# Local and pooled attention with a mixture layer on one core: eight output steps in whole float32, weight casts on another engine, and a planner with new rules

## The chip, the cores and the metric

The kernel runs on one core of one Trainium2 chip. Its engines work in parallel, each through its own queue in order: TensorE (PE, matmuls; PEld is its weight load), VectorE (DVE), ScalarE (ACT), GpSimd (POOL, which also issues the adding DMAs) and SyncE (SP, which issues the other DMAs). The metric is the device time of one execution in microseconds, as the median of several runs. Lower is better.

## The reference: what is computed

```python
# q, k, v: 8 batches, 8 heads, 576 tokens, 64 values
q_d, k_d, v_d = means over groups of 4 tokens                     # 144 pooled tokens
out_up = repeat(softmax(q_d k_d^T / 8) v_d, 4)                    # pooled attention
out_local = softmax(q k^T / 8 where |i - j| < 4) v                # local attention
x = (out_up + out_local), heads side by side                      # 4608 x 512
h = x @ w_in                                                      # 512 x 2048
P = a0 + a1 h + a2 h^2 + a3 h^3
Q = 1 + |b0| |h| + |b1| h^2
out = (P / (Q + 1e-6)) @ w_out                                    # 2048 x 512
```

Everything is float32.

## The kernel before, in words

**Attention.** A pair is two heads of a batch, so a batch is four pairs. For each pair the kernel multiplies q and k in ten windows of 58 tokens (L409) and for the pooled tokens (L426), takes exponentials on ScalarE (L456, L482), normalizes, turns the weights (L530, L537), multiplies them with v (L579, L568) and adds the two results into x, stored transposed (L611).

**The layer.** Tokens are taken in ten blocks: eight of 512 tokens, one batch each, and two that gather the last 64 tokens of four batches. The first block has 16 steps. A step takes 128 of the 2048 columns: it multiplies x with a chunk of w_in into a PSUM bank (`h_part`), ScalarE and VectorE form the rational function g = P / Q (`middle`), and two steps later g is multiplied with a chunk of w_out, into four banks that collect over the steps (`o_part`). A float32 value is split into a high part of reduced precision and a rest, and a product is three matmuls: high x high, rest x high, high x rest. Only the first block's product with w_in, L680, is done in whole float32, since the splits aren't ready there. `middle` forms 1/Q as exp(-ln Q), multiplies (L729) and then finds the rest of g in three further operations (L732, L737, L738).

**The weights.** Both matrices come as 32 chunks of 512 KB. Each is loaded into a buffer (a "spot"), scaled on ScalarE (L320), put together from two words on VectorE (L323, L326), and then split by `parts`: GpSimd rounds it to the high part (L340), VectorE subtracts to get the rest (L343). For w_out this happens directly after the decoding. The spots lie over memory whose owner isn't in use yet; there are five for the first chunks, four that rotate, and two more.

**What sets the order.** A planner: every piece of work is a task with an engine, a cost, what it reads and writes, and sometimes a due time. The planner works out for each task how late it may start, and then runs the engines in time. On each engine it takes, of the tasks whose inputs are there, the one that may start latest the soonest. The order that results is each engine's program. So constants such as `H0`, `H_FIRST` and `SPLIT_EARLY` are wishes that set the order; they are no waits. Before the first product, TensorE is given matmuls without use (L889) where the plan has it idle.

In the first block everything meets: batch 0's attention, the loading and splitting of both matrices, the 16 steps, and batch 1's attention, whose x the second block needs. From the second block on, a step is 24 matmuls on TensorE, and the attention of a later batch is woven in.

Of the kernel before, what the change touches and what calls it, by code (L numbers as in the profile page):

```python
# [72 lines left out]
class Task:  # L73
    __slots__ = ("engine", "dur", "fn", "due", "preds", "succs", "late", "start", "end", "n", "lag")


class Plan:

    LAG = {"PE": 0.25, "DVE": 0.14, "ACT": 0.18, "POOL": 0.2, "SP": 2.0}
    OWN = {"PE": 0.0, "DVE": 0.08, "ACT": 0.1, "POOL": 0.1, "SP": 2.0}
# [6 lines left out]
    def add(self, engine, dur, fn, reads=(), writes=(), due=None, lag=None):  # L89
        t = Task()  # L90
        t.engine, t.dur, t.fn, t.due, t.n = engine, dur, fn, due, len(self.tasks)
        t.lag, t.preds, t.succs, t.late, t.start = lag, {}, [], 1e9, None
# [11 lines left out]
        for k in rk - wk:  # L104
            self.readers[k].append(t) if k in self.readers else self.readers.__setitem__(k, [t])
# [62 lines left out]
def attention_moe(  # L168
# [95 lines left out]
    slots += [Slot(2 + i, high[i][half].at) for i in range(2)]  # L264
    vf = put("vf", [KC, NPAIR, 2, 2, D], F32, low[0][half].at)
# [3 lines left out]
    spots += [put(f"sl{i}", [P, 2 * DM], I32, a[w][NFC - 2].at) for i, (a, w) in enumerate(((high, 0), (low, 0), (high, 1), (low, 1)))]  # L269
    spots += [put(f"sx{i}", [P, 2 * DM], I32, xs[1][0].at + i * 4096) for i in range(2)]  # L270
# [34 lines left out]
    def weights(w, f, spot, due=None):  # L305
# [25 lines left out]
        add("SP", 1.4, load, (), (spot,), due=due)  # L331
# [3 lines left out]
        if w:  # L335
            parts(w, f)

    def parts(w, f, due=None):
        hi, lo, word = high[w][f], low[w][f], bits[w][f]
        add("POOL", 1.0, lambda: nc.gpsimd.tensor_copy(out=hi.ap, in_=word.ap.bitcast(F32)), (lo,), (hi,), due=due)  # L340
# [19 lines left out]
    def load_qk(c, due=None):  # L360
        s, b, i = c.slot, c.b, c.i
        add("SP", 1.6, lambda: nc.sync.dma_start(out=s.qk.ap, in_=qk[b, i]), (), (s.qk,), due=due)

# [4 lines left out]
    def load_pooled(c):

        s, b, i = c.slot, c.b, c.i  # L370
        for dst, src, cost in ((s.pq, qkp, 0.5), (c.vp, vp, 0.4)):
            add("SP", cost, lambda d=dst, x=src: nc.sync.dma_start(out=d.ap, in_=x[b, 0, :, i]), (), (dst,))
            for r in range(1, POOL):
                add(
                    "POOL", 1.0,
# [15 lines left out]
    def scores(c, bk):  # L391
# [24 lines left out]
        add("PE", 1.0, issue, (s.qk, identb, maskb), bk)  # L416

    def scores_pooled(cs, bk):
# [14 lines left out]
        add("PE", 0.9, issue, [c.slot.pq for c in cs], bk)  # L433
# [548 lines left out]
```

## Time and profile before

| what | value |
|---|---|
| median of 3 runs | 995.44 us (995.34 to 995.81) |
| span of the profiled execution | 992.7 us (its first to its last instruction; the timed runs' median is 2.7 us above it) |
| TensorE busy | 961.0 us, 97% |
| VectorE busy | 849.1 us, 86% |
| ScalarE busy | 796.6 us, 80% |
| GpSimd busy | 180.4 us, 18% |
| TensorE busy in 0 to 50, 50 to 100, 200 to 250 us | 35.0, 44.2, 50.0 us |
| VectorE busy in the same stretches | 35.4, 47.6, 44.8 us |
| mean granted TensorE clock | 0.995 |

The page gives the profiled execution by its span; what lies around the span is read as the difference to the median. A matmul on float32 operands appears as two records, so the 64 matmuls of L680 are 128 records. The ends of matmuls are modelled, and a matmul that waits in the array counts as busy; the cost of one is read from the distance between starts.

### The profile page before, as it was taken

To read this page: it belongs to the slowest core of one execution; us is meant where nothing else is said; L and a number is where in the kernel's file an instruction comes from. 1 tells how busy PE (TensorE), PEld (TensorE's weight loads), DVE (VectorE), ACT (ScalarE), POOL (GpSimd) and SP (SyncE) were. 2 spreads that over 40 slices of the span, in tenths; PEclk is the share of its full clock that TensorE was granted. 3 is DMA by queue.
4 is the path that set the end of the run, shared out by engine and by line. 5 is a ranking of instruction groups with operands and counts; after the bars stand their busy time and mean duration, and the time that the engine had idled before them with its cause. 6 is when DMAs were issued, how large, how long until landed. Compare 5 with 4: busy or idle time off the path is not lost.

```text
span 992.7 us, 19799 instructions
## 1 busy us (share of the span) xinstructions
PE 961.0 (97%) x7365; PEld 758.1 (76%) x7365; DVE 849.1 (86%) x1472; ACT 796.6 (80%) x2046; POOL 180.4 (18%) x209
## 2 busy tenths in 40 slices
PE   6689998999999999999999999999999999999997
PEld 5545665788888878987878887887878888898886
DVE  6799999989778988887887898888888898888886
ACT  6578768797979798779787988798797979767675
POOL 1523543222221213001303030302122220000000
PEclk9999999999999999999999999999999999999999
DMA  9963553433342324002424242533334320100001
GB/s 322 281 210 120 118 158 70 117 68 74 74 125 51 74 74 84 34 22 74 75 72 96 85 80 59 95 96 56 92 57 112 74 52 1 44 1 22 1 1 42
DMA packets 46371, 83.43 MB, mean 84 GB/s; under 512 B 6564, under 2 KB 29092, under 8 KB 46276
## 3 DMA queue, kind: packets, MB, share of 16 engines
q1 hardware_dynamic: 25828, 62.70, 19.1%
q0 software_dynamic: 20448, 19.48, 14.1%
q8 instruction: 58, 0.95, 0.4%
q14 instruction: 37, 0.30, 0.1%
HBM read 72.72 MB, written 9.44 MB: 83 GB/s over the span
## 4 chain that ended last, share of the span: by engine, by line
PE 82%; DVE 10%; DMA 4%; issue 2%; POOL 1%; SPq 1%; ACT 1%; ACTq 0%; DVEq 0%; POOLq 0%
PE psum L757 36%; PE psum L692 36%; PE psum L568 2%; DMA pq<-in_qkp_dram 2%; PE psum L579 1%; PE psum L530 1%; PE psum L537 1%; PE psum L409 1%; PE psum L426 1%; DMA qk<-in_qk_dram 1%; DVE m L720 1%; DMA sx<-in_w_out_dram 1%; DVE m L726 1%; POOL wh L340 1%; DVE g L729 1%
## 5 line engine op out<-in xcount | busy, mean ns | idle before, releaser
L757 PE MATMUL psum<-wh,g 128*128 128x512 f32 x1152 | 371.7, 403 | 4.7 <-DVE g L738 2.7
L692 PE MATMUL psum<-xs,wh 128*128 128x512 f32 (+1 forms) x1152 | 265.2, 370 | 0.0
L705 ACT ACTIVATE m<-psum,cf 128x512 f32<-128x512 f32 x288 | 217.5, 759 | 51.9 <-PE psum L692 41.9
L757 PEld LDWEIGHTS psum<-wh,g 128*128 128x128 f32 x1152 | 209.3, 188 | 55.5 <-issue 7.7
L692 PEld LDWEIGHTS psum<-xs,wh 128*128 128x128 f32 x1152 | 199.3, 188 | 35.9
L757 PE MATMUL psum<-wl,g 128*128 128x512 f32 x576 | 225.0, 392 | 0.0
L705 ACT ACTIVATE gb<-psum,cf 128x512 f32<-128x512 f32 x144 | 115.7, 803 | 53.9 <-PE psum L757 53.7
L376 POOL DMA_DIRECT2D pq<-in_qkp_dram x84 | 73.9, 913 | 398.3 <-DMA pq<-in_qkp_dram 312.5
L692 PE MATMUL psum<-xs,wl 128*128 128x512 f32 (+1 forms) x576 | 141.5, 367 | 0.0
L729 DVE TENSOR_TENSOR g<-m,m 128x512 fp32r<-128x512 f32 x144 | 100.6, 699 | 43.2 <-ACT m L705 41.3
L720 DVE SCALAR_TENSOR_TENSOR m<-m,cf,m 128x512 f32<-128x512 f32 x144 | 108.9, 756 | 31.2 <-ACT m L705 31.1
L757 PEld LDWEIGHTS psum<-wl,g 128*128 128x128 f32 x576 | 108.4, 188 | 23.4
L456 ACT ACTIVATE el<-psum,nm 128x64 f32<-128x64 f32 x320 | 97.0, 345 | 30.4 <-DVE nm L448 30.1
L726 DVE TENSOR_TENSOR m<-m,gb 128x512 f32<-128x512 f32 x144 | 101.7, 706 | 20.3 <-ACT gb L705 16.3
L692 PEld LDWEIGHTS psum<-xs,wl 128*128 128x128 f32 x576 | 101.3, 189 | 18.9 <-issue 1.2
L705 ACT ACTIVATE gb<-m,cf 128x512 f32<-128x512 f32 x144 | 107.0, 743 | 6.3 <-DVE m L720 6.3
L732 DVE SCALAR_TENSOR_TENSOR m<-m,g 128x512 f32<-128x512 f32 x144 | 100.0, 695 | 2.9
L737 DVE TENSOR_TENSOR m<-m,m 128x512 f32<-128x512 f32 x144 | 99.2, 689 | 2.8
L376 POOL DMA_DIRECT2D vp<-in_vp_dram x84 | 72.7, 925 | 154.5 <-DMA vp<-in_vp_dram 136.8
L725 DVE TENSOR_TENSOR m<-m,m 128x512 f32<-128x512 f32 x144 | 98.5, 684 | 0.5 <-ACT m L705 0.5
L738 DVE TENSOR_TENSOR g<-m,m 128x512 fp32r<-128x512 f32 x144 | 97.9, 680 | 0.8
L705 ACT ACTIVATE m<-gb 128x512 f32<-128x512 f32 x144 | 93.6, 650 | 3.5 <-DVE m L725 0.9
(66 smaller groups left out, 999.0 us busy)
## 6 DMA issues: line engine op xcount, KB each, us to landing
qk<-in_qk_dram SPq DMA_DIRECT2D x32, 590.0 KB, 8.0
pq<-in_qkp_dram POOLq DMA_DIRECT2D x84, 144.0 KB, 3.3
vw<-in_vw_dram SPq DMA_DIRECT2D x32, 320.0 KB, 4.0
out_dram<-xf SPq DMA_DIRECT2D x32, 256.0 KB, 2.4
vp<-in_vp_dram POOLq DMA_DIRECT2D x84, 72.0 KB, 3.0
sl<-in_w_in_dram SPq DMA_DIRECT2D x10, 512.0 KB, 4.7
sl<-in_w_out_dram SPq DMA_DIRECT2D x10, 512.0 KB, 6.3
pq<-in_qkp_dram SPq DMA_DIRECT2D x28, 144.0 KB, 2.2
```

The costliest lines, as they stand in the source:

```text
L376: lambda d=dst, x=src, r=r: nc.gpsimd.dma_start(out=d.ap, in_=x[b, r, :, i], accum_op=ALU.add),
L456: nc.scalar.activation(out=s.el.ap[:, k, c.pos(j), :], in_=view[:, j, k, :], func=AF.Exp, bias=nm[:, 5 * j + k : 5 * j + k + 1], scale=sca ...
L692: nc.tensor.matmul(ph.ap[:, f * t : (f + 1) * t], lhsT=(high, low)[j][0][fc].ap[:, c, :], rhs=blk.x[i].ap[:, c, :], start=(part_ == 0 and ...
L705: add("ACT", cost, lambda: nc.scalar.activation(out=out_.ap, in_=in_, func=func, **kw), (room_in, cf, *more), (out_,))
L720: lambda: v.scalar_tensor_tensor(out=tb.ap, in0=tq.ap, scalar=b1, in1=tb.ap, op0=ALU.mult, op1=ALU.add),
L725: add("DVE", 0.61, lambda: v.tensor_tensor(out=ta.ap, in0=ta.ap, in1=tq.ap, op=ALU.mult), (ta, tq), (ta,))
L726: add("DVE", 0.61, lambda: v.tensor_tensor(out=ta.ap, in0=ta.ap, in1=u.ap, op=ALU.add), (ta, u), (ta,))
L729: add("DVE", 0.61, lambda: v.tensor_tensor(out=gh.ap, in0=ta.ap, in1=tq.ap, op=ALU.mult), (ta, tq), (gh,))
L732: lambda: v.scalar_tensor_tensor(out=tb.ap, in0=tb.ap, scalar=CONE, in1=gh.ap.bitcast(F32), op0=ALU.add, op1=ALU.mult),
L737: add("DVE", 0.61, lambda: v.tensor_tensor(out=tb.ap, in0=ta.ap, in1=tb.ap, op=ALU.subtract), (ta, tb), (tb,))
L738: add("DVE", 0.61, lambda: v.tensor_tensor(out=gl.ap, in0=tb.ap, in1=tq.ap, op=ALU.mult), (tb, tq), (gl,))
L757: nc.tensor.matmul(ob[sub].ap, lhsT=g[i].ap[:, f0 : f0 + P], rhs=flat((high, low)[j][1][fc].ap), start=(fc == 0 and m == 0), stop=(fc == N ...
```

## The change

1. **Eight output steps in whole float32** (`WHOLE = 8`). In the first eight steps of the first block `middle` takes exp(-ln Q) as a first value of the reciprocal, refines it by one Newton step (two operations), and multiplies P with it: three operations after the reciprocal in place of four, with one float32 result in `u`. `o_part` multiplies it with the unsplit chunk of w_out, one float32 matmul for each of the four groups of 128 tokens in place of three. The first eight chunks of w_out are split after that, for the second block.
2. **The rounding of weights** moves from GpSimd (L340) to ScalarE.
3. **The planner** has a new rule: before it starts a task, it looks for a more urgent one that becomes ready while that task would run, and then holds the engine free or runs only what fits (`HOLD`, until `HOLD_UNTIL`). Loads have a landing time by their size. Many constants change.
4. **Batch 0** goes pair by pair through its attention, in place of two pairs at a time, with banks from a table (`FIRST`). Its pooled values of v are loaded into two buffers of two parts each, in place of one with four additions in a row, so L579's product has four terms in place of two there. Loads have no due times: all of batch 0 first, then the weights. Batch 1's loads are held back in the plan (`HOLD_LOADS`).
5. **Spots.** The two additional ones are gone, and the four rotating ones lie elsewhere.

```diff
     def parts(w, f, due=None):
-        add("POOL", 1.0, lambda: nc.gpsimd.tensor_copy(out=hi.ap, in_=word.ap.bitcast(F32)), (lo,), (hi,), due=due)
+        add("ACT", 0.5, lambda: nc.scalar.copy(out=hi.ap, in_=word.ap.bitcast(F32)), (lo,), (hi,), due=due)
...
-        if w:
+        if w and f >= WHOLE:
             parts(w, f)
...
         act(0.54, tq, log, log.ap, AF.Exp, scale=-1.0)
+        if n < WHOLE:
+            add("DVE", 0.61, lambda: v.scalar_tensor_tensor(
+                    out=tb.ap, in0=tb.ap, scalar=CONE, in1=tq.ap, op0=ALU.add, op1=ALU.mult), (tb, tq), (tb,))
+            add("DVE", 0.61, lambda: v.scalar_tensor_tensor(
+                    out=tq.ap, in0=tb.ap, scalar=2.0, in1=tq.ap, op0=ALU.subtract, op1=ALU.mult, reverse0=True
+                ), (tb, tq), (tq,))
+            add("DVE", 0.61, lambda: v.tensor_tensor(out=u.ap, in0=ta.ap, in1=tq.ap, op=ALU.mult), (ta, tq), (u,))
+            return
...
     def o_part(n, f):
+        if n < WHOLE:
+            x = gb[n % 2]
+            for sub in range(blk.nsub):
+                def issue(sub=sub):
+                    nc.tensor.matmul(
+                        ob[sub].ap, lhsT=x.ap[:, sub * P : (sub + 1) * P], rhs=flat(bits[1][fc].ap).bitcast(F32),
+                        start=(fc == 0), stop=False,
+                    )
+                add("PE", 0.858, issue, (x, low[1][fc]), (ob[sub],), due=due + 0.02 * sub)
+            return
...
-            t = heapq.heappop(open_[e])[2]
+            t = ready[e][0][2]
+            urgent = None
+            for r, _, w in waiting[e]:
+                if r < at + t.dur * HOLD and w.late < t.late - HOLD_MARGIN and (urgent is None or w.late < urgent[0]):
+                    urgent = w.late, r
+            if urgent is not None and at < HOLD_UNTIL:
+                fits = [x for x in ready[e] if at + x[2].dur <= urgent[1] + 0.05]
+                if not fits:
+                    free[e] = urgent[1]
+                    continue
...
-H0 = 40.0
-H_FIRST = 8.0
+H0 = 36.0
+H_FIRST = 6.73
...
-SPLIT_EARLY = 6.0
+SPLIT_EARLY = 9.51
+PARTS_EARLY = 14.42
+PAIR_GAP = 3.53
+HOLD = 0.7
+HOLD_MARGIN = 2.06
+HOLD_UNTIL = 54.4
+WHOLE = 8
+HOLD_LOADS = (45.0, 75.0)
```

How this moves instructions shows best at the end of batch 0's attention. First ScalarE's queue, ahead of step 0 of the first block (L705 before, L720 now, whose first row reads the bank with h). `sl` and `sx` rows are scalings of loaded weights, `up` the pooled result of a pair, `ept` and `et` its turned weights. Before:

```order
L320 ACTIVATE sx0_233<-sx0_233 128x512
L543 COPY ept3_221<-psum 72x288 x2
L553 COPY et3_220<-psum 128x512
L554 COPY et3_220<-psum 128x128
L625 ACTIVATE up0_191<-psum 128x144
L625 ACTIVATE up1_192<-psum 128x144
L320 ACTIVATE sl1_230<-sl1_230 128x512
L320 ACTIVATE sl3_232<-sl3_232 128x512
L320 ACTIVATE sl2_231<-sl2_231 128x512
L320 ACTIVATE sl0_229<-sl0_229 128x512
L320 ACTIVATE sx1_234<-sx1_234 128x512
L705 ACTIVATE m2_166<-psum,cf_181 128x512
```

Now:

```order
L557 COPY ept3_221<-psum 72x288 x2
L567 COPY et3_220<-psum 128x512
L568 COPY et3_220<-psum 128x128
L334 ACTIVATE sl3_233<-sl3_233 128x512
L354 CAST wh1_2_74<-wb1_2_125 128x512
L354 CAST wh1_3_75<-wb1_3_127 128x512
L640 ACTIVATE up1_192<-psum 128x144
L334 ACTIVATE sl2_232<-sl2_232 128x512
L354 CAST wh1_4_76<-wb1_4_129 128x512
L334 ACTIVATE sl1_231<-sl1_231 128x512
L720 ACTIVATE m2_166<-psum,cf_181 128x512
```

Of the five scalings that stood in a row ahead of step 0, two are left behind the last pair's `up`; casts of weights stand between.

The same place on VectorE: L611 (now L626) adds a pair's results into x, which the first product waits for; L323 and L326 (now L337 and L340) decode weights, L343 (now L357) subtracts the high part that GpSimd (now ScalarE) rounded. Before:

```order
L326 SCALAR_TENSOR_TENSOR wb1_11_143<-sx1_234,wb1_11_143 128x512
L343 TENSOR_TENSOR wl1_1_122<-wb1_1_123,wh1_1_73 128x512
L343 TENSOR_TENSOR wl1_2_124<-wb1_2_125,wh1_2_74 128x512
L611 TENSOR_TENSOR xf0_1_155<-psum,up0_191 128x48
L611 TENSOR_TENSOR xf2_1_163<-psum,up0_191 128x64
L611 TENSOR_TENSOR xf0_1_155<-psum,up1_192 128x48
L611 TENSOR_TENSOR xf2_1_163<-psum,up1_192 128x64
L611 TENSOR_TENSOR xf0_1_155<-psum,up0_191 128x464
L611 TENSOR_TENSOR xf0_1_155<-psum,up1_192 128x464
L323 TENSOR_SCALAR wb1_3_127<-sl1_230 128x512
```

Now:

```order
L340 SCALAR_TENSOR_TENSOR wb1_3_127<-sl1_231,wb1_3_127 128x512
L337 TENSOR_SCALAR wb0_6_101<-sl0_230 128x512
L340 SCALAR_TENSOR_TENSOR wb0_6_101<-sl0_230,wb0_6_101 128x512
L337 TENSOR_SCALAR wb1_4_129<-sl3_233 128x512
L340 SCALAR_TENSOR_TENSOR wb1_4_129<-sl3_233,wb1_4_129 128x512
L626 TENSOR_TENSOR xf0_1_155<-psum,up1_192 128x48
L626 TENSOR_TENSOR xf2_1_163<-psum,up1_192 128x64
L626 TENSOR_TENSOR xf0_1_155<-psum,up1_192 128x464
L337 TENSOR_SCALAR wb0_7_103<-sl2_232 128x512
```

The subtractions that wait for a cast are no longer ahead of the sums; in their place stand decodes of the second round of loads. The first subtraction now stands inside step 0.

More of the change, by code (lines that the diff above doesn't have):

```diff
@@ L73 @@
 class Task:
-    __slots__ = ("engine", "dur", "fn", "due", "preds", "succs", "late", "start", "end", "n", "lag")
+    __slots__ = ("engine", "dur", "fn", "due", "preds", "succs", "late", "start", "end", "n", "load", "at")
 class Plan:
-    LAG = {"PE": 0.25, "DVE": 0.14, "ACT": 0.18, "POOL": 0.2, "SP": 2.0}
-    OWN = {"PE": 0.0, "DVE": 0.08, "ACT": 0.1, "POOL": 0.1, "SP": 2.0}
+    ENGINES = ("PE", "DVE", "ACT", "POOL", "SP")
+    LAG = {"PE": 0.25, "DVE": 0.14, "ACT": 0.18, "POOL": 0.2}
+    OWN = {"PE": 0.0, "DVE": 0.08, "ACT": 0.1, "POOL": 0.1}
     def __init__(self):
@@ L112, in gap @@
     def gap(self, p, t):
-        if p.lag is not None:
-            return p.lag
+        if p.load is not None:
+            return 2.05 if p.engine == "SP" else 1.8 + 1.3 * p.load
         return (self.OWN if p.engine == t.engine else self.LAG)[p.engine]
@@ L263, in attention_moe @@
     half = NFC // 2
-    slots += [Slot(2 + i, high[i][half].at) for i in range(2)]
-    vf = put("vf", [KC, NPAIR, 2, 2, D], F32, low[0][half].at)
+    slots += [Slot(2 + i, high[i][half - 1].at) for i in range(2)]
+    vf = [put(f"vf{i}", [KC, NPAIR, 2, 2, D], F32, low[0][half + 2 * i].at) for i in range(2)]
     arena = nc.alloc_sbuf_tensor("arena", [P, (top - base) // 4 + 16], I32)
@@ L431, in issue @@
                         )
-        add("PE", 0.9, issue, [c.slot.pq for c in cs], bk)
+        add("PE", 1.02, issue, [c.slot.pq for c in cs], bk)
     def softmax_local(c, bk):
@@ L787, in store @@
                     ),
-                    (room,), (), due=due + 2,
+                    (room,), (), due=due + 2, load=0.7,
                 )
     order = sorted(((w, f) for w in range(2) for f in range(NFC)), key=lambda c: c[1] / 2 + 1.5 * c[0])
-    spot_of = [spots[i % 9] for i in range(9)] + [spots[5 + i % 4] for i in range(len(order) - 9)]
-    late = [i for i, (w, f) in enumerate(order) if f >= NFC - 2]
-    for n, i in enumerate(range(late[0], len(order))):
-        spot_of[i] = spots[9 + n % 2]
@@ L833, in attention_moe @@
-    for w, f, spot in chunks[len(early) :]:
+    chunks = [(w, f, spots[i if i < 9 else 5 + (i - 9) % 4]) for i, (w, f) in enumerate(order)]
+    c0 = [Pair(p) for p in range(NPAIR)]
+    for c in c0:
+        load_qk(c)
+    for r in range(POOL):
+        v = vf[r // 2]
+        if r % 2:
+            add(
+                "POOL", 0.93, lambda r=r, v=v: nc.gpsimd.dma_start(out=v.ap, in_=vp[0, r], accum_op=ALU.add),
+                (v,), (v,), load=1.3,
+            )
+        else:
+            add("SP", 0.8, lambda r=r, v=v: nc.sync.dma_start(out=v.ap, in_=vp[0, r]), (), (v,), load=0.8)
```

144 lines of the change are left out of this document (75 added, 69 removed), and 4 rows, old and new, of the table FIRST.

## The prediction

> **What bounds the kernel now.** I read the table of stages first, with the cuts where the work itself changes hands: at the first matmul of the first block (47.03), at the first polynomial operation on VectorE of that block (57.70), and at the same operation of the second block (183.60). The columns are busy time and instructions of each engine, then TensorE's granted clock and the DMA share.
>
> ```profile
> span 992.7 us, 19799 instructions
> 47.03:57.70 10.67, 9.64 (x60) 4.29 (x60) 7.85 (x14) 4.53 (x8) 3.02 (x4) 0.84 1.05 329
> 57.70:183.60 125.90, 115.68 (x731) 72.02 (x732) 123.62 (x216) 97.21 (x254) 48.74 (x49) 0.99 0.47 121
> 183.60:290.00 106.40, 106.40 (x892) 85.51 (x891) 92.10 (x165) 91.05 (x252) 19.75 (x23) 1.00 0.37 85
> ```
>
> From 183.60 on, TensorE is busy in every microsecond. In the first block it is not: there VectorE is busy 123.62 of 125.90, or 98%, and ScalarE 77%. So the first block is set by VectorE, the rest by TensorE, and the first 57 us by neither. The cuts are these rows of the timeline (start, duration):
>
> ```profile
> 47.03 8.80 PE L680 MATMUL psum<-xf,wb 128*128 128x512 f32 x16 [3.89 <-DVE xf L611]
> 57.70 0.75 DVE L720 SCALAR_TENSOR_TENSOR m<-m,cf,m 128x512 f32<-128x512 f32 x1
> 178.56 2.88 PE L692 MATMUL psum<-xs,wh 128*128 128x512 f32 x12
> 183.60 0.75 DVE L720 SCALAR_TENSOR_TENSOR m<-m,cf,m 128x512 f32<-128x512 f32 x1
> ```
>
> Next, what made the first polynomial so late. These are ScalarE's rows from its first exponential on; in brackets stands its idle time and what ended it.
>
> ```profile
> 8.65 0.31 ACT L456 ACTIVATE el<-psum,nm 128x64 f32<-128x64 f32 x1 [6.64 <-DVE nm L448]
> ...
> 47.61 0.67 ACT L320 ACTIVATE sl<-sl 128x512 f32<-128x512 f32 x1 [5.28 <-DMA sl<-in_w_out_dram]
> 50.62 0.68 ACT L320 ACTIVATE sl<-sl 128x512 f32<-128x512 f32 x1 [2.34 <-DMA sl<-in_w_out_dram]
> 51.91 0.70 ACT L320 ACTIVATE sl<-sl 128x512 f32<-128x512 f32 x1 [0.61 <-DMA sl<-in_w_in_dram]
> 53.82 0.70 ACT L320 ACTIVATE sl<-sl 128x512 f32<-128x512 f32 x1 [1.21 <-DMA sl<-in_w_in_dram]
> 55.91 0.70 ACT L320 ACTIVATE sx<-sx 128x512 f32<-128x512 f32 x1 [1.40 <-DMA sx<-in_w_out_dram]
> 56.52 0.66 ACT L705 ACTIVATE m<-psum,cf 128x512 f32<-128x512 f32 x1
> ```
>
> ScalarE stood 10.84 us (5.28 + 2.34 + 0.61 + 1.21 + 1.40) before five weight scalings that are queued ahead of step 0, each waiting for its load. Those loads left late because VectorE had not yet decoded what lay in their buffers.
>
> Last, what makes VectorE so full. GpSimd rounds weights to the high part (L340), and VectorE's operation beside such a cast is stretched: 3.17 beside a run of five, 1.09 beside one, 0.74 or 0.68 alone. The third and fourth rows are one pair, the last two the last pair of the block.
>
> ```profile
> 59.11 3.23 POOL L340 CAST wh<-wb 128x512 fp32r<-128x512 f32 x5
> 59.72 3.17 DVE L726 TENSOR_TENSOR m<-m,gb 128x512 f32<-128x512 f32 x1
> 70.05 1.01 POOL L340 CAST wh<-wb 128x512 fp32r<-128x512 f32 x1 [7.71 <-DVE wb L326]
> 70.51 1.09 DVE L720 SCALAR_TENSOR_TENSOR m<-m,cf,m 128x512 f32<-128x512 f32 x1
> 75.89 0.74 DVE L720 SCALAR_TENSOR_TENSOR m<-m,cf,m 128x512 f32<-128x512 f32 x1
> 161.95 0.94 POOL L340 CAST wh<-wb 128x512 fp32r<-128x512 f32 x1
> 161.81 1.64 DVE L729 TENSOR_TENSOR g<-m,m 128x512 fp32r<-128x512 f32 x1
> L340 POOL CAST wh<-wb 128x512 fp32r<-128x512 f32 x24 | 28.8, 1284 | 45.0 <-DVE wb L326 45.0
> ```
>
> Between 57.70 and 183.60 there are 24 such casts and 15 stretched operations, the first at 59.72 and the last at 161.81; their excess over the usual length of their kind adds up to 8.4 us (2.48 in the first, 0.95 in the last, 0.34 to 0.41 in each of the others).
>
> **The change part by part.** *TensorE, the output product.* The prices are in these rows: weight loads of the whole-float32 matmul start 0.43 apart (five steps from 59.60 to 61.74), two to a matmul, so 0.857 each; twelve split matmuls take 2.72, so 0.227 each.
>
> ```profile
> 59.60 0.19 PEld L680 LDWEIGHTS psum<-xf,wb 128*128 128x128 f32 x1 [0.24 <-issue]
> 61.74 0.19 PEld L680 LDWEIGHTS psum<-xf,wb 128*128 128x128 f32 x1 [0.24 <-issue]
> 242.01 2.72 PE psum L757 x12
> ```
>
> A step's twelve split matmuls (2.72) become four whole ones (3.43): +0.71, eight times, +5.7 us of TensorE. The price is that of L680, the same operand types and sizes. Batch 0's pooled values come in two halves, which doubles 16 small matmuls, about +2. All of this falls before the second block, where TensorE has room: by the count of its queue at these prices, 110 us lie between 47.03 and 178.56, a stretch of 131.5. The changed queue has 110 again from the first product that needs pair 3 to the second block: the +5.7 is there, but six of the eight matmuls of steps 0 and 1 (5.1) have moved ahead of it, among the attention of pairs 2 and 3. As long as VectorE needs more than that, the addition is covered and costs nothing; without that cover it costs up to 7.7.
>
> *VectorE.* Between its first polynomial operations of block one and of block two the queue held 215 instructions and now holds 216: 8 fewer in the steps (six instead of seven, eight times, at a spacing of 0.61, -4.9), 10 more subtractions of weight parts (L343 at 0.60, six that stood in the head and four from the second block, +6.0), one decode fewer (-0.6): +0.5. The spacing is read from neighbours that run back to back:
>
> ```profile
> 65.96 0.68 DVE L737 TENSOR_TENSOR m<-m,m 128x512 f32<-128x512 f32 x1
> 66.56 0.68 DVE L726 TENSOR_TENSOR m<-m,gb 128x512 f32<-128x512 f32 x1
> 67.16 0.68 DVE L738 TENSOR_TENSOR g<-m,m 128x512 fp32r<-128x512 f32 x1
> ```
>
> The casts leave GpSimd, so the 8.4 go. VectorE needs 123.6 + 0.5 - 8.4 = 115.7 us.
>
> *ScalarE* gets the casts: 26 in this interval. The nearest row is its own cast of the same shape:
>
> ```profile
> L659 ACT CAST xs<-xf 128x512 fp32r<-128x512 f32 (+1 forms) x36 | 19.6, 575 | 9.2 <-DVE xf L611 8.7
> 10.00:20.00 10.00, 7.56 (x166) 5.51 (x155) 7.95 (x18) 8.92 (x56) 1.43 (x2) 1.00 1.04 369
> 20.00:30.00 10.00, 6.79 (x70) 4.99 (x70) 6.71 (x16) 8.88 (x50) 1.45 (x2) 1.00 1.05 356
> 30.00:40.00 10.00, 9.02 (x146) 7.20 (x146) 8.66 (x21) 8.57 (x21) 3.89 (x6) 1.00 1.02 296
> ```
>
> 26 at 0.52 to 0.575 and one more scaling (0.6) make +14.1: 111.3 of busy time against 97.2. In that interval it has 28.7 idle, so it is hidden, but no longer by much.
>
> *The interval.* VectorE at 100% would give 115.7, its present length is 125.9. With ScalarE and TensorE now within 5% of VectorE, I expect a little more waiting than the 2% of before: 96%, 120.6.
>
> *The head.* ScalarE paces it. From 8.65 to 56.52 it was busy about 32 us (26.4 of them in the three stages above, at 88%) and idle 16. Ahead of step 0 the changed queue has six casts more (+3.4) and one scaling fewer (-0.6): 34.8. The scalings that waited at 47 to 56 belong to loads that now leave sooner, because their buffers' decodes stand ahead of the last pair's sums and no longer beside a queue that waits for GpSimd. At 88% busy, 34.8 take 39.5: step 0 reaches ScalarE at 8.65 + 39.5 = 48.2 and VectorE 1.2 later (57.70 - 56.52), at 49.4. Bounds: 46.5 (95% busy) and 57.7 (all five waits return).
>
> *Sum.* The second block's first polynomial comes at 49.4 + 120.6 = 170.0 in place of 183.60, -13.6. What TensorE has left from there on is 0.7 more by the queues' count. 992.7 - 13.6 + 0.7 = 979.8 for the profiled span. The timed runs' median, 995.44, lies 2.7 above the span: **982.5**.
>
> *A rule against it.* TensorE's clock was 0.84 in the stage 47.03 to 57.70, after the 3.89 of idle in the first timeline row; it lost 0.16 x 10.67 = 1.7 us. The changed queue has 47 warming matmuls of L889's kind in place of 101. The Trainium skill ("TensorE: Matmul & The Clock Gate", the part on the HAM clock gate) says that an idle window of about 3.4 us puts the array at half rate until it has been busy as long; the trace agrees with that row. By that rule the thinner warming could bring two or three such falls into the head, an estimate of 3 to 5 us, and the sum would be 986 to 988; by the row, where TensorE was 50 to 75% busy at clock 1.00 from 10 to 40, there is none. I stay with the row.
>
> **The rivals.** *The loads stay late.* ScalarE and VectorE are queues in order, and four rotating buffers replace six; each load still waits for a decode. For it: the five waits above. Against it: the DMA share falls after the head. Then the first polynomial stays at 57.70 and only the interval shortens: 57.7 + 120.6 = 178.3, 992.7 - 5.3 + 0.7 = 988.1, timed 990.8.
>
> *More than I say.* 46.5 + 115.7 = 162.2: 992.7 - 21.4 + 0.7 = 972.0, timed 974.7. Against it: three engines at 93 to 100% in order.
>
> *Batch 1 arrives no sooner.* The second block needs batch 1's attention, whose second half ended at these waits:
>
> ```profile
> 165.00 0.48 PE L530 MATMUL psum<-ident,ep 112*72 112x112 f32 x3 [1.34 <-ACT et L553]
> 174.49 1.27 PE L568 MATMUL psum<-et,vw 64*64 64x58 f32 x64 [1.02 <-ACT m L705]
> ```
>
> If its pooled loads, chained three deep on GpSimd, come when they came, block two starts when it did: 993.4, timed 996.1, no change. Against it: GpSimd loses the casts that stood between its transfers.
>
> *Slower: ScalarE becomes the bound.* Its 111.3 in the interval is the largest growth of any engine. If the 28.7 of idle stay, because a cast or scaling queued ahead of a step holds the polynomial behind it, the interval is 140.0: 49.4 + 140.0 = 189.4, 992.7 + 5.8 + 0.7 = 999.2, timed 1001.9. It decides for slower once ScalarE idles more than about 24 us there (183.6 - 49.4 - 0.7 + 2.0 - 111.3). Against it: most of that idle was waiting for a VectorE that was slower.
>
> **How the numbers follow.** The forecast has 0.62, with its own range 976 to 990 (first polynomial 46.5 to 53, interval 117 to 124); late loads 0.12; more gain 0.08; batch 1 no sooner 0.08; ScalarE 0.10. A difference under 0.2%, 2.0 us, cannot be told from none here, so faster (below 993.4) is 0.62 + 0.12 + 0.08 = 0.82, the same 0.08, slower 0.10. Leaving out the slow case, most of the no-change case and the end of the largest gain gives 975 to 992.
>
> **What would show it.** Right: VectorE's first polynomial near 49, the second block's near 170, no stretched VectorE operation beside a GpSimd cast, ScalarE about 90% busy in between, whole-float32 output matmuls 0.857 apart, and TensorE full from the second block on. Wrong: ScalarE idle for loads before step 0, TensorE or ScalarE gaps that add up to over 10 us in the first block, or gaps of TensorE after it, where ScalarE's and VectorE's work per block is unchanged within 4 us.

## The result and the profile after

| | before | changed |
|---|---|---|
| median | 995.39 us (992.11 to 995.81, 4 runs) | **985.36 us** (984.52 to 986.79, 4 runs) |
| span of the profiled execution | 992.7 us | 985.0 us |
| ratio of the times | | 0.9912, 95% interval 0.9890 to 0.9934 |

The change makes the kernel 10.0 us faster, 0.9%. The profiled execution of the changed kernel took 986.79 us, the slowest of its four. First the table of stages of the changed kernel, cut at the same two operations as before (first polynomial operation on VectorE of the first and of the second block). The columns are busy time and instructions of TensorE, its weight load, VectorE, ScalarE and GpSimd, then TensorE's granted clock, the DMA share and GB/s.

```profile
span 985.0 us, 19666 instructions
0.00:53.31 53.31, 40.58 (x555) 29.13 (x555) 36.55 (x81) 37.00 (x149) 2.52 (x8) 0.94 0.75 254
53.31:175.99 122.68, 119.24 (x744) 65.97 (x745) 117.06 (x217) 110.23 (x282) 31.63 (x36) 1.00 0.60 159
175.99:282.39 106.40, 106.40 (x853) 85.52 (x852) 91.53 (x163) 91.36 (x245) 20.63 (x24) 1.00 0.35 80
```

The head is 4.39 shorter (57.70 before), the first block 3.22 (125.90), and what follows the second block's first polynomial takes 809.0 (985.0 - 175.99) against 809.1. All of the gain lies ahead of 176 us. In the first block VectorE has 6.6 less to do, ScalarE 13.0 more.

The waits of ScalarE's scalings ahead of step 0 are short now. They are these rows of the timeline of the changed kernel (start, duration, idle time and what ended it):

```profile
42.93 0.67 ACT L334 ACTIVATE sl<-sl 128x512 f32<-128x512 f32 x1 [0.29 <-DMA sl<-in_w_out_dram]
44.80 0.69 ACT L334 ACTIVATE sl<-sl 128x512 f32<-128x512 f32 x1 [0.69 <-DMA sl<-in_w_in_dram]
49.31 0.67 ACT L334 ACTIVATE sl<-sl 128x512 f32<-128x512 f32 x1 [0.17 <-DMA sl<-in_w_in_dram]
51.54 0.67 ACT L334 ACTIVATE sl<-sl 128x512 f32<-128x512 f32 x1 [1.06 <-DMA sl<-in_w_out_dram]
```

Together 2.2 us in place of 10.84. Which of the change's parts brings the loads sooner (the order, the spots, the loads' own order) was not tested one by one. But the head has a hole that was not there before. The table of stages of the changed kernel shows it, for ten microseconds and then for single ones at its two ends:

```profile
20.00:30.00 10.00, 8.78 (x84) 6.93 (x85) 4.18 (x11) 6.65 (x27) 0.00 (x0) 0.66 1.00 399
19.00:20.00 1.00, 0.00 (x1) 0.00 (x0) 1.00 (x2) 1.00 (x7) 0.00 (x0) 1.00 1.05 341
20.00:21.00 1.00, 0.00 (x0) 0.00 (x0) 0.61 (x3) 1.00 (x6) 0.00 (x0) 0.58 1.02 407
26.00:27.00 1.00, 1.00 (x7) 0.66 (x7) 0.00 (x0) 1.00 (x4) 0.00 (x0) 0.51 0.99 389
27.00:28.00 1.00, 1.00 (x16) 0.80 (x16) 0.23 (x1) 1.00 (x3) 0.00 (x0) 1.00 0.96 389
```

The timeline of the changed kernel at the same place, with the engines' rows as they start:

```profile
20.48 0.69 ACT L557 COPY ept<-psum 72x288 f32<-72x288 f32 x2
21.22 2.93 PE L924 MATMUL psum<-maskb,identb 128*128 128x256 bf16 x13 [2.22 <-ACT ept L557]
24.37 1.32 PE L544 MATMUL psum<-ident,ep 112*72 112x112 f32 x6
24.40 0.59 ACT L567 COPY et<-psum 128x512 f32<-128x512 f32 x1 [1.75 <-PE psum L551]
27.77 0.61 DVE L485 TENSOR_REDUCE nm<-psum 128x3 f32<-128x432 f32 x1 [5.32 <-ACT st L334]
```

TensorE stood from 19.0 to 21.22, because thirteen warming matmuls write a bank that ScalarE's copy (L557) had yet to read. Its clock was 0.5 from 20.2 to 27.0, in all 6.8 us. The warming matmuls took 2.93, and ScalarE (1.75) and VectorE (5.32) waited behind.

The chain of waits in the first block has changed its nature as well. In the kernel before (start, length, what) it is VectorE's almost throughout until 167.1, and TensorE's behind that: of the 126 us 88.4 are VectorE's by the sum of its rows, 15.5 TensorE's, 12.3 short stretches without a releaser (issue), and 8.9 are three runs of casts on GpSimd like this one:

```profile
85.72 2.90 POOL wh L340
```

In the changed kernel the same view passes from engine to engine; these are rows at which it changes hands, and the one by which it ends:

```profile
67.37 5.89 DMA sl<-in_w_out_dram
73.87 1.12 ACT wh L354 x2
...
98.10 0.54 ACT m L720
...
110.89 6.83 DMA sl<-in_w_in_dram
...
136.10 3.63 PE psum L695 x8
...
171.62 4.53 PE psum L707 x20
```

Read in full, it is VectorE until 67.3, a weight load (sent when VectorE has decoded what lay in its buffer), ScalarE from 73.9 to 98.6, VectorE until 110.8, a second load, ScalarE and VectorE in turn until 135, and from 135 to 176 TensorE alone. TensorE holds a third of it (40.9 us), VectorE and ScalarE about a quarter each (32.5 and 32.0), and the two loads 12.7.

### The profile page after: what moved, and what is told of

Read it like the earlier page. It is cut to its first block, busy times and chain, and to the rows that moved or that the text cites. A ratio compares the mean times of both kernels' runs of the same rounds, so it can differ in the third digit from the quotient of the medians.

```text
span 985.0 us, 19666 instructions
## 1 busy us (share of the span) xinstructions
PE 963.5 (98%) x7311; PEld 752.1 (76%) x7311; DVE 833.4 (85%) x1464; ACT 812.1 (82%) x2078; POOL 147.6 (15%) x176
## 4 chain that ended last, share of the span: by engine, by line
PE 87%; ACT 5%; DVE 5%; DMA 3%; issue 1%; SPq 0%; ACTq 0%; DVEq 0%
PE psum L802 38%; PE psum L707 37%; PE psum L582 2%; PE psum L544 2%; PE psum L594 2%; PE psum L551 2%; ACT el L470 2%; PE psum L423 1%; PE psum L695 1%; PE psum L440 1%; DMA sl<-in_w_out_dram 1%; DMA qk<-in_qk_dram 1%; ACT m L720 1%; DMA sl<-in_w_in_dram 1%; PE psum L413 1%
## 5 line engine op out<-in xcount | busy, mean ns | idle before, releaser
L802 PE MATMUL psum<-wh,g 128*128 128x512 f32 x1088 | 345.6, 399 | 0.1
L720 ACT ACTIVATE m<-psum,cf 128x512 f32<-128x512 f32 x288 | 218.1, 757 | 60.8 <-PE psum L707 60.3
L802 PEld LDWEIGHTS psum<-wh,g 128*128 128x128 f32 x1088 | 197.6, 188 | 43.6 <-issue 3.1
L802 PE MATMUL psum<-wl,g 128*128 128x512 f32 x544 | 212.0, 391 | 0.0
L720 ACT ACTIVATE gb<-psum,cf 128x512 f32<-128x512 f32 x144 | 115.8, 804 | 55.6 <-PE psum L802 55.6
L390 POOL DMA_DIRECT2D pq<-in_qkp_dram x84 | 73.9, 917 | 482.0 <-DMA pq<-in_qkp_dram 359.0
L762 DVE TENSOR_TENSOR g<-m,m 128x512 fp32r<-128x512 f32 x136 | 93.8, 690 | 50.6 <-ACT m L720 48.6
L741 DVE TENSOR_TENSOR m<-m,gb 128x512 f32<-128x512 f32 x144 | 99.1, 688 | 25.3 <-ACT gb L720 21.7
L802 PEld LDWEIGHTS psum<-wl,g 128*128 128x128 f32 x544 | 102.1, 188 | 22.5
L720 ACT ACTIVATE gb<-m,cf 128x512 f32<-128x512 f32 x144 | 107.6, 747 | 0.8 <-DVE m L735 0.8
L740 DVE TENSOR_TENSOR m<-m,m 128x512 f32<-128x512 f32 x144 | 98.5, 684 | 2.0 <-ACT m L720 2.0
L765 DVE SCALAR_TENSOR_TENSOR m<-m,g 128x512 f32<-128x512 f32 x136 | 93.8, 690 | 3.2
L720 ACT ACTIVATE m<-gb 128x512 f32<-128x512 f32 x144 | 93.0, 646 | 4.0 <-DVE m L740 1.1
L770 DVE TENSOR_TENSOR m<-m,m 128x512 f32<-128x512 f32 x136 | 93.6, 688 | 2.3
L771 DVE TENSOR_TENSOR g<-m,m 128x512 fp32r<-128x512 f32 x136 | 92.5, 680 | 0.7
```

Source lines behind the costliest of these rows:

```text
L390: lambda d=dst, x=src, r=r: nc.gpsimd.dma_start(out=d.ap, in_=x[b, r, :, i], accum_op=ALU.add),
L720: add("ACT", cost, lambda: nc.scalar.activation(out=out_.ap, in_=in_, func=func, **kw), (room_in, cf, *more), (out_,))
L740: add("DVE", 0.61, lambda: v.tensor_tensor(out=ta.ap, in0=ta.ap, in1=tq.ap, op=ALU.mult), (ta, tq), (ta,))
L741: add("DVE", 0.61, lambda: v.tensor_tensor(out=ta.ap, in0=ta.ap, in1=u.ap, op=ALU.add), (ta, u), (ta,))
L762: add("DVE", 0.61, lambda: v.tensor_tensor(out=gh.ap, in0=ta.ap, in1=tq.ap, op=ALU.mult), (ta, tq), (gh,))
L765: lambda: v.scalar_tensor_tensor(out=tb.ap, in0=tb.ap, scalar=CONE, in1=gh.ap.bitcast(F32), op0=ALU.add, op1=ALU.mult),
```

## The experiments

All are timed beside the kernel before on the same chip (its medians in the four sets of runs were 995.33, 995.11, 994.84 and 994.09 us). "Step 0" is the first polynomial operation, "interval" the stretch to the second block's, both of one profiled execution. The order of instructions is the changed kernel's except in e2, e3, e4 and e9, where the planner was run anew. How far two executions of one block can differ is seen in e7, the changed kernel and e8: their first blocks hold the same instructions in the same order and took 123.85, 122.68 and 121.63. A difference of an interval below some 2 us is therefore not shown by one execution.

| run | time, us | ratio, 95% | step 0 | interval |
|---|---|---|---|---|
| changed | 985.36 | 0.9912 (0.9890 to 0.9934) | 53.31 | 122.68 |
| e1, casts on GpSimd | 1000.47 | 1.0048 (1.0031 to 1.0065) | 53.53 | 136.49 |
| e2, no whole-float32 output steps | 983.48 | 0.9878 (0.9862 to 0.9895) | 52.43 | 116.94 |
| e3, before with casts on ScalarE | 990.88 | 0.9955 (0.9940 to 0.9970) | 56.84 | 122.30 |
| e4, before with whole-float32 steps | 997.93 | 1.0028 (1.0019 to 1.0037) | 61.72 | 126.38 |
| e5, TensorE 4.9 lighter by its price | 986.15 | 0.9912 (0.9893 to 0.9930) | 51.89 | 121.62 |
| e6, VectorE 4.4 lighter by its price | 986.62 | 0.9915 (0.9900 to 0.9930) | 54.65 | 121.21 |
| e10, both | 987.10 | 0.9924 (0.9911 to 0.9938) | 57.18 | 120.70 |
| e12, both and ScalarE lighter | 983.84 | 0.9902 (0.9886 to 0.9919) | 52.37 | 119.88 |
| e11, ScalarE 16 heavier | 1002.82 | 1.0082 (1.0069 to 1.0096) | 56.90 | 134.78 |
| e7, thirteen warming matmuls out | 987.41 | 0.9934 (0.9914 to 0.9954) | 52.53 | 123.85 |
| e8, the thirteen into bank 5 | 984.16 | 0.9894 (0.9878 to 0.9910) | 50.91 | 121.63 |
| e9, e2 and e8 together | **980.32** | 0.9854 (0.9839 to 0.9869) | 48.97 | 117.10 |

### e1: the changed kernel with the casts back on GpSimd

```diff
-        add("ACT", 0.5, lambda: nc.scalar.copy(out=hi.ap, in_=word.ap.bitcast(F32)), (lo,), (hi,), due=due)
+        add("ACT", 0.5, lambda: nc.gpsimd.tensor_copy(out=hi.ap, in_=word.ap.bitcast(F32)), (lo,), (hi,), due=due)
```

The planner still books ScalarE, so the order on the other engines stays.

> The changed kernel with one difference: the 32 roundings of weights run on GpSimd again, at the places where the plan has them for ScalarE, so that the order on every other engine stays word for word. Theory (the stretched VectorE operations were worth 8 us): some 26 casts fall between the first polynomial operations of block one and block two, each stretches one VectorE operation by about 0.35 to 0.4, VectorE's busy time there goes from 117 to about 126, and the time from 985.4 to 990 to 993. Rival (ScalarE bounds the changed block as much as VectorE does): the 14 us that ScalarE loses pay for the stretches, 983 to 987.

Measured 15.1 us more than the changed kernel, and more than either expectation. The table of stages of e1:

```profile
53.53:190.02 136.49, 125.28 (x745) 69.02 (x745) 132.63 (x217) 99.45 (x256) 58.84 (x62) 0.96 0.56 143
```

One group of e1 in that stretch (instructions, then busy time, mean ns of one and idle time before):

```profile
L357 DVE TENSOR_TENSOR wl<-wb,wh 128x512 fp32r<-128x512 f32 x32 | 26.5, 832 | 1.0 <-POOL wh L354 1.0
```

Two rows of its timeline:

```profile
105.33 2.12 DVE L337 TENSOR_SCALAR wb<-sl 128x512 int32<-128x512 int32 x1
105.67 1.49 POOL L354 CAST wh<-wb 128x512 fp32r<-128x512 f32 x2
```

And that group in the changed kernel's interval, with the one of 105.33:

```profile
L357 DVE TENSOR_TENSOR wl<-wb,wh 128x512 fp32r<-128x512 f32 x32 | 21.7, 684 | 0.1
L337 DVE TENSOR_SCALAR wb<-sl 128x512 int32<-128x512 int32 x18 | 7.3, 423 | 1.4 <-ACT sl L334 1.4
```

The same 217 VectorE instructions take 132.63 in place of 117.06: 15.6 for 26 casts, 0.60 each, and the interval follows with 13.8. So the stretching is real and comes from the casts, but it is no fixed price. Here casts also run two and more in a row, and what VectorE does at that time is held up: the operation of 105.33 took 2.12 where its kind takes 0.42 on average. The Trainium skill ("SBUF — State Buffer", the part on who interferes with whom) says that VectorE and GpSimd share a pair of ports as an exclusive lock, so that one of them blocks for the length of the other's instruction. The size of that row, its own 0.42 and two casts' 1.49 and more, agrees; the stretch of 0.35 beside the single cast of 70.05 in the kernel before (1.09 in place of 0.74, with 0.55 of the cast still to run) is less than a full block.

### e3: the kernel before with the casts on ScalarE

```diff
-        add("POOL", 1.0, lambda: nc.gpsimd.tensor_copy(out=hi.ap, in_=word.ap.bitcast(F32)), (lo,), (hi,), due=due)
+        add("ACT", 0.5, lambda: nc.scalar.copy(out=hi.ap, in_=word.ap.bitcast(F32)), (lo,), (hi,), due=due)
```

> The kernel before with one difference: the roundings of weights go to ScalarE. Theory: VectorE's interval from block one to block two loses its 8.4 us of stretch, and the head loses VectorE's waits for GpSimd: 995.4 goes to 985 to 989. Rival (the gain needs the planner's new order): 992 to 996, with ScalarE's casts holding back its own steps.

Measured 4.5 us less than before, between the two expectations' ranges. The table of stages of e3:

```profile
56.84:179.14 122.30, 115.64 (x727) 73.37 (x728) 117.11 (x218) 105.53 (x274) 20.82 (x24) 0.96 0.47 122
```

VectorE falls from 123.62 to 117.11 and the interval from 125.90 to 122.30. In the old order the casts' move alone takes 3.6 off the interval, more than the changed kernel's whole 3.2. (The planner was run anew, and VectorE has 218 instructions there in place of 216.) Of the head's 4.4 it gives 0.9; the others come from the rest of the change (order, spots, loads), whose parts were not separated.

### e2 and e4: the whole-float32 steps taken out, or alone

e2 sets one constant of the changed kernel; e4 puts the changed branches of `middle`, `o_part` and the late splitting into the kernel before, with the casts left on GpSimd.

```diff
-WHOLE = 8
+WHOLE = 0
```

> The changed kernel with no step in whole float32 (all products with w_out in three split matmuls, g split by four operations in every step); the planner, the casts on ScalarE and batch 0's order stay. Theory (VectorE sets the first block, TensorE's addition is covered): VectorE +4.9 us there, TensorE -5.7, the time 3 to 5 us longer, 988 to 990. Rival (TensorE sets it now): 3 to 6 us shorter, 980 to 982.

> The kernel before with one difference: the first eight output steps in whole float32, with g from the refined reciprocal, and the first eight chunks of w_out split afterwards; casts stay on GpSimd. Theory: VectorE's interval loses 4.9 us and some subtractions go to the second block, the 5.7 us of TensorE are covered: 989 to 992. Rival (TensorE's addition is exposed): 998 to 1001.

Both say that this part costs time. Without it the changed kernel is 1.9 us faster (the ranges of the two ratios overlap), and added to the kernel before it makes that 2.6 us slower. The table of stages of e2, first block and then second:

```profile
52.43:169.37 116.94, 113.29 (x812) 71.01 (x813) 112.79 (x211) 110.12 (x283) 31.22 (x36) 1.00 0.69 179
169.37:275.77 106.40, 104.33 (x801) 83.60 (x800) 95.42 (x172) 89.39 (x242) 20.58 (x24) 1.00 0.34 74
```

The interval is 5.7 shorter, the length that the eight steps add to TensorE. But of that, 3.4 comes back: after the second block's start e2 takes 812.4 (981.8 - 169.37) in place of 809.0, as subtractions fall into the second block (VectorE 95.42 there, 91.53 in the changed kernel) and TensorE has 2.1 of gaps in its first 106 us. Interval and rest together make 2.3. e4's loss lies in its head, whose first polynomial came at 61.72; why the planner's new order is late there was not followed further.

### e5, e6, e10: one engine lighter, the order kept

e5 narrows seven of the eight steps' output matmuls, e6 the first of the added VectorE operations, e10 does both. They leave out that part of the computation.

```diff
+            wide = 512 if n == 0 else 408
...
-                        ob[sub].ap, lhsT=x.ap[:, sub * P : (sub + 1) * P], rhs=flat(bits[1][fc].ap).bitcast(F32),
+                        ob[sub].ap[:, :wide], lhsT=x.ap[:, sub * P : (sub + 1) * P],
+                        rhs=flat(bits[1][fc].ap).bitcast(F32)[:, :wide],
...
-                    out=tb.ap, in0=tb.ap, scalar=CONE, in1=tq.ap, op0=ALU.add, op1=ALU.mult
+                    out=tb.ap[:, :8], in0=tb.ap[:, :8], scalar=CONE, in1=tq.ap[:, :8], op0=ALU.add, op1=ALU.mult
```

> The changed kernel with every queue in its order; in steps 1 to 7 the whole-float32 product with w_out takes 408 of the 512 columns, so that one costs 0.68, the price of three split matmuls, in place of 0.857 (28 matmuls, 4.9 us of TensorE less; the last 104 columns of these seven chunks are left out of the sum). Theory now (TensorE's addition is exposed, as the two runs without and with it suggest): 2 to 5 us shorter, 980 to 983. Rival (VectorE alone sets the block, and what the whole-float32 steps cost comes from where the subtractions of weights went): no change, 984.5 to 986.5.

> The changed kernel with every queue in its order; the first of the three new operations (Q times the first reciprocal) treats 8 of 512 columns in each of the eight steps, about 0.55 less each, 4.4 us of VectorE; the refinement is left out in the other columns. Theory of the prediction (VectorE sets the block): 3 to 4.4 us shorter, 981 to 982.5. Rival (TensorE and ScalarE set it as much): under 2 us, 983.5 to 985.5.

> The two cuts of e5 and e6 together, with the order kept: the output product of steps 1 to 7 takes 408 of 512 columns (TensorE 4.9 less) and the first added VectorE operation of each of the eight steps takes 8 of 512 columns (VectorE 4.4 less); the outputs of these steps are not the reference's. Alone, each shortened the interval of 122.7 by no more than 1.5. If TensorE and VectorE hold the interval together, each covering the other's gain, the two cuts give more than the sum of the single ones: 4 to 5, an interval near 118 and a time near 982. If something third (ScalarE's queue, or the chain through one step) sets it, the interval stays at 120 to 121.5 and the time at 985.

The times stay at the changed kernel's, and the intervals shrink by 1.1, 1.5 and 2.0, no more than equal blocks differ. VectorE's busy time fell by 3.2 in e6. Neither engine alone sets the first block, and e10 gives nothing near the 4 to 5 that were expected if the two covered each other. The stages of e10 show both cuts, and a head that was later than in any other execution of this order:

```profile
0.00:57.18 57.18, 44.38 (x555) 31.27 (x555) 36.64 (x80) 36.85 (x149) 2.51 (x8) 0.88 0.75 246
57.18:177.88 120.70, 115.75 (x745) 66.49 (x745) 113.61 (x217) 110.32 (x282) 32.28 (x36) 0.99 0.61 156
```

The chain of the changed kernel says why. The matmuls that e5 narrows end there by about 120 us (the last eight records start at 116.76 in its timeline), and from 135 on TensorE alone holds the chain.

### e11 and e12: ScalarE heavier and lighter, the order kept

```diff
-        add("ACT", 0.5, lambda: nc.scalar.copy(out=hi.ap, in_=word.ap.bitcast(F32)), (lo,), (hi,), due=due)
+        def cast():
+            nc.scalar.copy(out=hi.ap, in_=word.ap.bitcast(F32))
+            nc.scalar.copy(out=hi.ap, in_=word.ap.bitcast(F32))
+
+        add("ACT", 0.5, cast, (lo,), (hi,), due=due)
```

e12 is e10 with ScalarE's third polynomial line in steps 2 to 15 on 8 of 512 columns.

```diff
-        act(0.66, ta, h, h.ap, AF.Identity, scale=a3, bias=a2)
+        cut = 8 if 2 <= n < 16 else 512
+        add("ACT", 0.66, lambda: nc.scalar.activation(out=ta.ap[:, :cut], in_=h.ap[:, :cut], func=AF.Identity, scale=a3, bias=a2), (h, cf), (ta,))
```

> Each cast of weight parts is done twice on ScalarE, with the order of all else kept: ScalarE gets 26 more casts of about 0.52 in the interval (+13.7) and six or so more in the head (+3). ScalarE is idle 12.4 of 122.7 there. If ScalarE is the third that holds the interval (its queue decides), every cast added lengthens it: interval about 134, head 56, time near 999. If the idle is real room, the interval grows by 1.5 to 3 (123.9 of work in 125) and the head by up to 3: 988 to 991.

> As e10 (TensorE 4.9 and VectorE 4.4 lighter, interval 120.7), and ScalarE lighter too, with the order kept: in steps 2 to 15 the ScalarE operation that makes the third coefficient line (Identity, 128x512) takes 8 of 512 columns, so the outputs are not the reference's. It is not on the chain of its step that ends last; fourteen times about 0.45 is 6.3 of ScalarE. e11 lengthened the interval by 12.1 for 16.0 more of ScalarE, 0.76 for 1. If ScalarE's queue sets the interval, that holds downwards: 4 to 5 less, an interval near 116 and a time near 982. If ScalarE had room and e11 only used it up, nothing goes: interval 120 to 121, time as e10's 987.

Upwards, ScalarE counts for three quarters: 16.0 more busy time lengthen the interval by 12.1 and the time by 17.5 (a part of it is the head's, 3.6, where this execution had 6.8 us more at half clock). The chain of waits in e11's interval is ScalarE's for 84.7 of 134.8. Downwards it doesn't: 5.1 less shorten the interval by 0.8 against e10. The stages of e11:

```profile
56.90:191.68 134.78, 124.12 (x745) 67.34 (x745) 118.01 (x216) 126.25 (x308) 31.59 (x36) 0.97 0.56 143
```

and of e12:

```profile
52.37:172.25 119.88, 114.03 (x745) 66.10 (x745) 112.98 (x218) 105.25 (x282) 31.27 (x36) 1.00 0.64 163
```

What ScalarE waited for in the interval of e12 (total, times, longest):

```profile
ACT sl L334 <- DMA sl<-in_w_out_dram: 4.1, 2, 2.9
ACT gb L720 <- PE psum L811: 3.8, 1, 3.8
ACT m L720 <- PE psum L707: 2.4, 1, 2.4
ACT sl L334 <- DMA sl<-in_w_in_dram: 1.9, 2, 1.0
```

The same waits in the changed kernel:

```profile
ACT gb L720 <- PE psum L802: 3.2, 1, 3.2
ACT sl L334 <- DMA sl<-in_w_in_dram: 2.6, 2, 2.1
ACT m L720 <- PE psum L707: 2.4, 1, 2.4
ACT sl L334 <- DMA sl<-in_w_out_dram: 2.0, 1, 2.0
```

The waits grew from 10.2 in the changed kernel (the four added up) to 12.2. Against e10, by the rows of the stages, ScalarE's idle time grew from 10.4 to 14.6: of the 5.1 that it saves, it waits 4.3. So in the changed kernel little of ScalarE's idle time is room. It lies in a few holes, ahead of weight loads and of TensorE, and a task added elsewhere in the queue delays the end. The first block stands where the three engines and the loads nearly balance: making ScalarE (e11) or VectorE (e1) heavier costs most of its size, making one lighter gives little. e12's 3.3 us in the time against e10 go with the head (52.37 against 57.18 in the profiled executions), whose instructions are the same in both.

### e7, e8, e9: the hole in the head

e7 leaves out the thirteen warming matmuls, e8 lets them write bank 5, which is not in use at that time; e9 is e8 without the whole-float32 steps.

```diff
     def warm(n):
+        spare = banks[5 if n == 13 else 7]
         for _ in range(n):
-            nc.tensor.matmul(banks[7].ap[:, : 2 * P], lhsT=identb.ap, rhs=flat(maskb.ap)[:, : 2 * P], start=True, stop=True)
+            nc.tensor.matmul(spare.ap[:, : 2 * P], lhsT=identb.ap, rhs=flat(maskb.ap)[:, : 2 * P], start=True, stop=True)
```

> The changed kernel without the 13 warming matmuls at 21 us, which stand ahead of pair 0's last turn and wait for the same copy. Theory (the head is late by the queue of 13 at half clock, 2.9 us): step 0 about 2.5 us sooner, 982 to 983.5. Rival (the head is paced by ScalarE's queue and by loads): no change, 984.5 to 986.5. Third way (without them the half clock holds longer): 986 to 988.

> The changed kernel; the same 13 warming matmuls write bank 5, which nobody reads then, so that they run at 19 us and do not wait for the copy. Theory (TensorE's idle stretch from 19.0 to 21.2 let the clock fall to half from 20.4 to 27.2, and both the 13 and the half clock made the head late): clock 1.00 in the stage 20 to 30 in place of 0.66, step 0 at 49.5 to 51 in place of 53.3, 981 to 983. Rival (loads and ScalarE's queue pace the head): 984.5 to 986.5 at full clock.

> Both findings together: no whole-float32 output product (as e2, 983.5) and the thirteen warming matmuls into bank 5 (as e8, 984.2, which lay 1.2 below the changed kernel). If they add, the time is 982.3, the clock between 20 and 30 us is 1.00, step 0's first polynomial comes near 50.5 and the second block's near 167.5. Rival: e2's head (52.43) was already free of the fall's cost, or another wait takes the place of the one removed; then 983.5 as e2.

Without the matmuls the clock fell as well. The stage of e7:

```profile
20.00:30.00 10.00, 8.04 (x84) 6.28 (x84) 5.46 (x13) 7.99 (x35) 0.00 (x0) 0.66 1.00 395
```

With the other bank it didn't. The timeline of e8:

```profile
18.79 1.58 PE L925 MATMUL psum<-maskb,identb 128*128 128x256 bf16 x13
21.72 0.77 PE L544 MATMUL psum<-ident,ep 112*72 112x112 f32 x6
24.11 0.61 DVE L485 TENSOR_REDUCE nm<-psum 128x3 f32<-128x432 f32 x1 [1.71 <-PE psum L440]
```

and the same stage:

```profile
20.00:30.00 10.00, 9.09 (x148) 7.05 (x146) 7.43 (x19) 9.52 (x37) 0.00 (x0) 1.00 1.01 399
```

The thirteen run at 18.79 in 1.58 us, the following transposes begin 2.65 earlier (21.72 for 24.37), VectorE's reduction 3.66 earlier, and ScalarE is busy 9.52 of 10 in place of 6.65. Step 0 comes 2.4 earlier, with a shorter fall later in the head (0.83 from 40 to 50) that the changed kernel's execution did not have. In the time e8 gives 1.2, between theory and rival, and the ranges of its ratio and the changed kernel's overlap.

But the wait alone does not decide. In e5 the thirteen write bank 7 and wait as in the changed kernel, the head's order is the same, and the clock stayed at 1.00 there:

```profile
21.46 1.58 PE L926 MATMUL psum<-maskb,identb 128*128 128x256 bf16 x13 [2.21 <-ACT ept L557]
20.00:30.00 10.00, 8.54 (x133) 7.17 (x133) 6.57 (x17) 8.92 (x37) 0.00 (x0) 1.00 1.00 400
```

Of the eight profiled heads whose thirteen write bank 7, seven show a fall at this place; of the two with bank 5, none. The table gives, from stages of one microsecond, the time at half clock before step 0, and step 0 less half of that time:

| head | half clock, us | step 0 | step 0 less half of it |
|---|---|---|---|
| changed | 6.8 | 53.31 | 49.9 |
| e1 | 6.8 | 53.53 | 50.1 |
| e2 | 3.4 | 52.43 | 50.7 |
| e5 | 3.4 | 51.89 | 50.2 |
| e6 | 10.2 | 54.65 | 49.5 |
| e10 | 13.7 | 57.18 | 50.3 |
| e11 (six casts more) | 13.7 | 56.90 | 50.1 |
| e12 | 3.4 | 52.37 | 50.7 |
| e7, no thirteen | 6.8 | 52.53 | 49.1 |
| e8, bank 5 | 3.4 | 50.91 | 49.2 |
| e9, bank 5 | 0 | 48.97 | 49.0 |

The first column explains most of the spread of step 0 from 49 to 57 us. At equal clock the waiting thirteen cost about one microsecond (49.5 to 50.7 against 49.0 to 49.2), so of e8's 2.4 the larger part is one fall more or less.

e9 gives 3.2 against e2, with ranges of the ratios that overlap slightly. There the whole head runs at full clock, as its stages show:

```profile
0.00:48.97 48.97, 37.99 (x555) 26.91 (x555) 37.19 (x83) 35.53 (x147) 2.51 (x8) 1.00 0.78 264
48.97:166.07 117.10, 114.35 (x813) 71.74 (x813) 112.70 (x211) 109.98 (x283) 32.12 (x36) 0.99 0.67 176
```

e9, at 980.32 us, is faster than both kernels, 5.0 below the changed one. Leaving the thirteen out (e7, 987.26 to 989.83) is no better than the changed kernel. That warming matmuls which wait for nothing keep the clock up fits e8 and e9; two executions don't prove it.

## Why the prediction was right, and where not

Faster was forecast with 0.82, 982.5 us in a range of 975 to 992; it is 985.36, 2.9 above, with the mechanism in the main as described and two terms too small. The nearness of the number is in part luck. In the profiled execution the span is 5.2 above the forecast's 979.8 (985.0). Of that, 1.4 drops out of the time because the profiled execution was the slowest of the four, and 0.9 because the sum adds 2.7 from span to time, where every timed execution that lists both has 1.7 to 1.9.

- **Three stretches, and the sum over them.** It held. By the sum's own rule, 992.7 + (175.99 - 183.60) + 0.7 = 985.8, against a span of 985.0; the rest of the program moved by 0.1.
- **The loads ahead of step 0 come sooner.** It held: 2.2 us of waiting in place of 10.84. The rival "loads stay late" is out, since step 0 did not stay at 57.70.
- **The head, 49.4.** It was 53.31, 3.9 late, and the step that failed is "by the row ... there is none. I stay with the row". I argued from the kernel before, at full clock from 10 to 40, that thinner warming brings no fall, and I misread the rows: TensorE is 68 to 90% busy there (7.56, 6.79 and 9.02 of 10), and not 50 to 75%; the column beside it, the weight loads, has 50 to 72%. ScalarE's work was as forecast: from 8.65 to 52.20 it was busy 34.6, against 34.8. What the forecast lacked is a fall of 6.8 us, 3.4 of them lost, behind a wait of 2.22; that is most of the 3.9. What I did not do was to read what the warming matmuls wait for: they write bank 7, and the new table of banks puts transposes of pair 0 there, which ScalarE still had to copy. The Trainium skill ("TensorE: Matmul & The Clock Gate", the part on the HAM clock gate) has an idle window and then half rate until the array has been busy as long. It was right against my row that falls would come, and e5 shows that a wait of 2.2 brings one in some executions and not in others. The sum by that rule, 986 to 988 by my estimate, lay nearer to the 985.36 than mine. With no fall in the head (e9) step 0 stands at 48.97, 0.4 from the forecast's 49.4; e9's head has two ScalarE instructions fewer (147 against 149), so it is not quite the same.
- **No stretched VectorE operation.** It held: VectorE 117.06 against a forecast of 115.7. That the stretching comes from the casts is shown by e1 and e3. Its size is not a number of the casts: 6.5 us of VectorE in the old order (e3), 15.6 in the new (e1), where I had read 8.4. In the changed order the move was worth 15.1 us, and without it the change would have been slower than before.
- **The interval, 120.6.** It was 122.68; the size is close and the reason behind it was not. "VectorE at 96%" (it was 95.4%) is an arithmetic mean over a block in which VectorE holds the chain for 26%. e6 takes 3.2 of VectorE's busy time and gets 1.5 at most. The words "the addition is covered and costs nothing" for the +5.7 of TensorE are the second step that failed: e2 puts it at 5.7 of the interval, of which 3.4 comes back later, and 1.9 in the time. Against e8, e9 puts it at 3.8 in the time; in the profiled executions 1.2 of that is the block and what follows (4.5 of the interval, 3.4 back), and 1.9 the head, where e8 had a fall and e9 none. The cover was argued from sums over the block. From 135 us on there is none, for TensorE is the chain there. e5 shows only that matmuls cut before 120 us save nothing; that what costs is the moved order and not the matmuls themselves is argued, not shown.
- **ScalarE's casts are hidden.** Its busy time was forecast well (111.3, measured 110.23). "Hidden, but no longer by much" was right of the changed kernel only in the direction: e11 shows that 16.0 more lengthen the interval by 12.1, though 12.4 stood idle. The rival "ScalarE becomes the bound" was wrong as priced (12.4 idle, not 28.7), but one more change of the same size makes it true, and slower than before: 1002.82.
- **Batch 1 no sooner.** The second block's first polynomial came at 175.99 in place of 183.60; this rival is out. So is "more than I say": no execution of this order had its first step at 46.5 or an interval of 115.7.

## What to carry to other kernels

When several engines stand above 90% in a stage, the busiest one is not "the bound": read the chain of waits in that stage, see where it changes hands, and price an edit by the stretch it falls in. A matmul that is there only to keep the clock up should wait for nothing; check which bank it writes and who still reads that bank. And price a cast on GpSimd by what VectorE does at the same time, not by its own length, because the same cast cost VectorE about 0.3 us in one order (6.5 over 24) and 0.6 in another.

## What the runs showed of the hardware that was not expected

- A stand of TensorE of 2.2 us was followed by a clock of 0.5 for 6.8 us in the changed kernel, though TensorE was busy again from 21.2 on, for 3.4 us in e10, and for none in e5. Two heads with the same instructions in the same order had mean clocks of 0.94 (changed) and 0.88 (e10), and their first steps came at 53.31 and 57.18. The single stretches at half clock lasted 3.4, 6.8 or 10.2 us (the last in e10, from 45 on), that is once, twice or three times the same length. The later falls, from 40 us on, differ from execution to execution; what decides them stays open.
- Beside casts on GpSimd in a row even a VectorE operation with a single input was held up: 2.12 us (e1, 105.33) for one that takes 0.42 on average in the changed kernel.
- ScalarE, 10% idle over 123 us, took up only a quarter of 16 us more: 12.1 of 16.0 showed in the interval.
